# One section of the modulation weights by eight small transfers

## The chip, the cores and the metric

The kernel runs on one core of a Trainium2 chip. The metric is device time in microseconds of one execution. Before the change the median of three runs is 667.86 us (667.57 to 667.94).

## The reference

One decode step of a block with adaptive layernorm, for 4 rows (B = 4) of 512 values, all inputs in bf16. Attention has 32 heads of 128 over a cache of 4096 positions; the cache (K and V, 4 x 32 x 4096 x 128 each) is nearly all of the 283 MB read.

```
mod = silu(c) @ w_mod                       # w_mod: 512 x 3072, six sections of 512 columns
sa, ca, ga, sb, cb, gb = the six sections   # 4 x 512 each
h = layernorm(x) * (1 + ca) + sa
x = x + ga * (softmax((h @ wq) K^T / sqrt(128)) V @ wo)
h = layernorm(x) * (1 + cb) + sb
z = gelu(h @ w_in)                          # w_in: 512 x 1792
z1, z2 = halves of z;  z2 = layernorm(z2)
out = x + gb * ((z1 * (w_sp * z2 + b_sp)) @ w_out)   # w_out: 896 x 512
```

Section 4 of w_mod, cb, is the scale of the second norm.

## The kernel before

The 128 pairs of row and head are taken in 32 steps of four heads of one row. A step loads 4 MB of K and 4 MB of V, each partition holding 128 consecutive positions of one head. VectorE multiplies K by the query in two halves (mult, L288), PE sums over the head's dimension by matmuls with an identity (reduce_d, L294), VectorE finishes the scores (sum8 and scores), ScalarE takes the exponential (L326), PE multiplies with V two steps later (pv, L366). K tiles ("kt") and V tiles ("vt") have two buffers each. The schedule is manual: every engine takes its instructions in the order of the code.

All large loads are issued by SyncE in the order of the code, and its queue holds them in that order:

- at the start wq (L89), five sections of w_mod into wm_sb (L92), K of steps 0 and 1, V of step 0;
- in step i, K of step i+2 (load_k) and V of step i (load_v; V of step 1 is loaded in step 0), through the helper's line L104;
- after step 2's V: the four parts of wo (L581) and wo_last (L586), into the pool wts, which takes the memory of the pool pre (wq and wm_sb) when that is closed;
- in step 30: the last V in five parts (L104), win_sb (L597), wout_sb (L599, in wts) and the gate's section of w_mod, section 5 (L602), which goes into a buffer of the V tiles.

Small loads (c, x, and w_sp and b_sp into sp_t) are issued by ScalarE.

Before step 0, c is turned into columns by four transposes on PE (rows_to_cols, L187), silu is computed on these columns (L226 to L234) into cT, and mod_cols (L242) multiplies sections 0 and 1 of w_mod with cT for the first norm. In step 2, mod_cols multiplies sections 2, 3 and 4 (ga, sb, cb) into modT (L573). In step 5, the scalars of w_sp and b_sp are spread (L589 to L591) and 1 is added to cb (L593).

After the last step come the output projection, the second norm, the two halves of gate with win_sb (L684), the product with wout_sb (L707), the gate's section (L715), and one store (L753).

Of the kernel before, what the change touches and what calls it, by code (L numbers as in the profile page):

```python
# [8 lines left out]
BF16 = mybir.dt.bfloat16  # L9
F32 = mybir.dt.float32  # L10
AF = mybir.ActivationFunctionType
ALU = mybir.AluOpType
# [12 lines left out]
def kernel(  # L25
# [16 lines left out]
    nc = tc.nc  # L42
    P = 128
    B, _, D = A_x.shape
    _, H, SK, DH = A_k_cache.shape
    F = B_w_in.shape[1]
    FH = F // 2
    DJ = D // P
    NF = F // P
    NH = FH // P  # L50
    NJ = SK * HQ // P
# [13 lines left out]
    consts = ctx.enter_context(tc.tile_pool(name="consts", bufs=1))  # L65
    kvp = ctx.enter_context(tc.tile_pool(name="kv", bufs=2))
# [6 lines left out]
    def ps_sm(shape, dtype=F32):  # L73
        return psum.tile(shape, dtype, name="sm", bufs=3)
# [6 lines left out]
    pre = pre_cm.__enter__()  # L81
    c_sb = pre.tile([B, D], BF16, name="c_sb")
# [4 lines left out]

    wq_sb = pre.tile([P, DJ, H * DH], BF16, name="wq_sb")
    nc.sync.dma_start(out=wq_sb, in_=A_wq.rearrange("(p j) n -> p j n", p=P))  # L89
    wm_sb = pre.tile([P, DJ, 5 * D], BF16, name="wm_sb")  # L90
    wm = w_mod.rearrange("(p j) n -> p j n", p=P)
    nc.sync.dma_start(out=wm_sb, in_=wm[:, :, 0:5 * D])  # L92

    def kv_view(cache, i):
        g, b = divmod(i, B)
# [16 lines left out]
    def load_v(i):  # L112
# [8 lines left out]
    ident_bf = consts.tile([P, P], BF16, name="ident_bf")  # L121
# [13 lines left out]

    st2 = consts.tile([P, 2, DJ + 1], F32, name="st2")
    nc.vector.memset(st2, 0.0)
    nc.vector.memset(st2[:, 1, DJ:], LN_EPS * D / P)

# [3 lines left out]
        out=sel32, in_=ident_f.rearrange("p (q r) -> p r q", r=R), axis=AX.X, op=ALU.add  # L143
# [10 lines left out]
    for g in range(G):  # L154
        nc.vector.tensor_reduce(out=selg[:, g:g + 1], in_=idr[:, g], axis=AX.XY, op=ALU.add)
    nc.vector.tensor_reduce(
        out=sel4, in_=ident_f.rearrange("p (c b) -> p b c", b=B), axis=AX.X, op=ALU.add
# [3 lines left out]
        out=mask8, in_=ident_f.rearrange("p (h u) -> p h u", h=2 * HQ), axis=AX.X, op=ALU.add  # L161
# [3 lines left out]
    x1w = consts.tile([P, DJ, R], F32, name="x1w")  # L165
    nc.gpsimd.memset(x1w, 0.0)
    cT = consts.tile([P, DJ, B], BF16, name="cT")

    consts.tile([P, 512], mybir.dt.uint8, name="gap")
    wk.tile([P, 32], mybir.dt.uint8, name="gap", bufs=1)  # L170
    pbds, opss = [], []
    for k in range(3):
        t = consts.tile([P, NJ, HQ], BF16, name=f"pbd{k}")
        nc.gpsimd.memset(t, 0.0)
        pbds.append(t)
    for k in range(2):
        t = psum.tile([P, G, DH], F32, name=f"ops{k}", bufs=1)
# [3 lines left out]
    def bc(ap, n):  # L181
        return ap[:, None, :].to_broadcast([P, n, ap.shape[-1]])

    def rows_to_cols(src):
        t = ps_sm([P, DJ, B], BF16)
        for j in range(DJ):
            nc.tensor.transpose(t[:, j, :], src[0:B, j:D:DJ], ident_bf[0:B, 0:B])  # L187
        return t

    def across(rhs, mat):  # L190
# [13 lines left out]
    def normed(pool, src, name, then=None, last=None):  # L204
# [16 lines left out]
        rsqrt(rs, v, 1.0, eps)  # L221
        return xc, rs

    cps = rows_to_cols(c_sb)
    cx = pre.tile([P, DJ, B], F32, name="cx")
    nc.vector.tensor_copy(out=cx, in_=cps)  # L226
    sg = pre.tile([P, DJ, B], F32, name="sg")
    nc.vector.tensor_scalar(
        out=sg, in0=cx, scalar1=-60.0, scalar2=-1.0, op0=ALU.max, op1=ALU.mult
    )  # L230
    nc.scalar.activation(out=sg, in_=sg, func=AF.Exp)
    nc.vector.tensor_scalar_add(out=sg, in0=sg, scalar1=1.0)
    nc.vector.reciprocal(out=sg, in_=sg)
    nc.vector.tensor_tensor(out=cT, in0=cx, in1=sg, op=ALU.mult)  # L234

    def mod_cols(s0, n, dst):

        for m in range(n):
            s, j = divmod(m, DJ)
            c0 = (s0 + s) * D + j  # L240
            for k in range(DJ):
                nc.tensor.matmul(  # L242
                    dst[:, m, :], lhsT=wm_sb[:, k, c0:c0 + (P - 1) * DJ + 1:DJ], rhs=cT[:, k, :],
                    start=(k == 0), stop=(k == DJ - 1),
                )
# [11 lines left out]
        out=hs, in0=modA[:, DJ:2 * DJ, :], scalar=1.0, in1=xn, op0=ALU.add, op1=ALU.mult  # L257
# [174 lines left out]
    for n in set(SETS):  # L432
        picks[n] = consts.tile([P, n, P], BF16, name=f"pick{n}")
        for a in range(n):
            u = P // n
            nc.vector.tensor_copy(
                out=picks[n][:, :, a * u:(a + 1) * u],
                in_=ident_bf.rearrange("p (u r) -> p r u", r=n),
# [77 lines left out]
        nc.vector.tensor_tensor(out=a, in0=a, in1=wp, op=ALU.add)  # L516

    modT = consts.tile([P, 3 * DJ, B], F32, name="modT")

    g8 = consts.tile([P, 2, B], F32, name="g8")  # L520
    sp_t = consts.tile([1, 2], BF16, name="sp_t")
# [8 lines left out]
    for i in range(NT):  # L530
        more = list(QPLAN.get(i, ()))
        mult(i, 0)
        if i >= 1:
            scores(i - 1)
        if i >= 2:
            norm_b(i - 2)
        add_up()
        rows_up()
        dealt()
        if i >= 3:  # L540
            o_pick(i - 3)
        reduce_d(i, 0)
        if i >= 3:
            o_cols(i - 3)
        if more:
            queries(more.pop(0))
        mult(i, 1)
        if i >= 1:
            norm_r(i - 1)
        if i >= 3:  # L550
            o_scale(i - 3)
        sum8(i, 0)
        reduce_d(i, 1)
        load_k(i + 2)
        if i >= 1:
            norm_a(i - 1)
        project()
        if i - 3 in ends:
            deal(ends[i - 3])
        while more:  # L560
            queries(more.pop(0))
        if i >= 2:
            pv(i - 2)
        if i == 0:
            load_v(1)
        elif 2 <= i < L:
            load_v(i)
        if i == 2:
            nc.scalar.dma_start(out=sp_t[:, 0:1], in_=B_w_sp[0:1, 0:1])
            nc.scalar.dma_start(out=sp_t[:, 1:2], in_=B_b_sp.rearrange("(a b) -> a b", b=1))  # L570
            mps = ps_sm([P, 3 * DJ, B])
            mod_cols(2, 3 * DJ, mps)
            nc.vector.tensor_copy(out=modT, in_=mps)  # L573
            pre_cm.__exit__(None, None, None)
            wts = tl = ctx.enter_context(tc.tile_pool(name="wts", bufs=1))
            wo_sb = wts.tile([P, H - HQ, D], BF16, name="wo_sb")
            wo_last = wts.tile([P, HQ, D], BF16, name="wo_last")
            hl = (H - HQ) * DH
            h0 = 0
            for n in SETS:  # L580
                nc.sync.dma_start(  # L581
                    out=wo_sb[:, h0:h0 + n, :],
                    in_=A_wo[h0 * DH:(h0 + n) * DH].rearrange("(p r) n -> p r n", p=P),
                )
                h0 += n
            nc.sync.dma_start(out=wo_last, in_=A_wo[hl:H * DH].rearrange("(q p) n -> p q n", p=P))  # L586
        if i == 5:
            sps = ps_sm([P, 2])
            nc.tensor.matmul(sps, lhsT=ones_b, rhs=sp_t, start=True, stop=True)  # L589
            nc.vector.tensor_copy(out=spf, in_=sps)  # L590
            nc.vector.tensor_copy(out=g8[:, 1, :], in_=spf[:, 0:1].to_broadcast([P, B]))  # L591
            cbT = modT[:, 2 * DJ:3 * DJ, :]
            nc.vector.tensor_scalar_add(out=cbT, in0=cbT, scalar1=1.0)  # L593
        if i == L - 1:
            load_v(L)
            win_sb = wts.tile([P, DJ, F], BF16, name="win_sb")
            nc.sync.dma_start(out=win_sb, in_=B_w_in.rearrange("(p j) n -> p j n", p=P))  # L597
            wout_sb = wts.tile([P, NH, D], BF16, name="wout_sb")
            nc.sync.dma_start(out=wout_sb, in_=B_w_out.rearrange("(j p) n -> p j n", p=P))  # L599
            wg_sb = kvp.tile([P, NJ, DH], BF16, name="vt", bufs=2)  # L600
            wg_sb = wg_sb.rearrange("p n d -> p (n d)")[:, 0:DJ * D].rearrange("p (k n) -> p k n", k=DJ)
            nc.sync.dma_start(out=wg_sb, in_=wm[:, :, 5 * D:])  # L602

    gaT = modT[:, 0:DJ, :]
# [24 lines left out]
    def sums():  # L629
# [21 lines left out]
        out=nv2, in0=mq2[:, 0:1], scalar=mq2[:, 0:1], in1=mq2[:, 1:2],  # L651
        op0=ALU.mult, op1=ALU.subtract,
# [6 lines left out]
        out=hl, in0=xs, scalar=mq2[:, 0:1], in1=cbT[:, :, BL], op0=ALU.subtract, op1=ALU.mult  # L659
    )  # L660
    nc.vector.scalar_tensor_tensor(
        out=hT2[:, :, BL], in0=hl, scalar=rsl, in1=sbT[:, :, BL], op0=ALU.mult, op1=ALU.add
# [4 lines left out]
        out=x1m, in0=x1[:, :, :, None].to_broadcast([P, DJ, B, HQ]),  # L667
        in1=mask4[:, None, None, :].to_broadcast([P, DJ, B, HQ]), op=ALU.mult,
    )
    x1r = ps_sm([B * DJ, P])  # L670
    for k in range(DJ):
        nc.tensor.matmul(
            x1r[:, k:P:DJ], lhsT=x1m[:, k].rearrange("p b j -> p (b j)"), rhs=sel32,
            start=True, stop=True,
# [4 lines left out]
    def gate(h):  # L679
# [21 lines left out]
        out=zz.rearrange("p f g b -> p g b f"), in0=z1[:, None].to_broadcast([P, 2, B, NH]),  # L701
        in1=st3[:, 0:2], op=ALU.mult,
    )
    y = ps_q()[:, 0:DJ * 2 * B].rearrange("p (j g b) -> p j g b", j=DJ, g=2)
    for j in range(DJ):
        for f in range(NH):
            nc.tensor.matmul(  # L707
                y[:, j], lhsT=wout_sb[:, f, j * P:(j + 1) * P], rhs=zz[:, f],
                start=(f == 0), stop=(f == NH - 1),
# [3 lines left out]
    for j in range(DJ):  # L713
        for k in range(DJ):
            nc.tensor.matmul(  # L715
                gb[:, j, :], lhsT=wg_sb[:, k, j * P:(j + 1) * P], rhs=cT[:, k, :],
                start=(k == 0), stop=(k == DJ - 1),
# [3 lines left out]
        out=mq3, in_=ps3.rearrange("p (g b f) -> p g b f", g=2, b=B), axis=AX.X, op=ALU.add  # L721
# [4 lines left out]
        out=rs3, in0=mq3[:, 1], scalar=LN_EPS, in1=rs3, op0=ALU.add, op1=ALU.subtract  # L726
# [3 lines left out]
        out=g8[:, 0, :], in0=mq3[:, 0, :], scalar=-1.0, in1=g8[:, 1, :], op0=ALU.mult, op1=ALU.mult  # L730
# [5 lines left out]
        out=t3[:, 2], in0=yb[:, 0], scalar1=spf[:, 1:2], scalar2=None, op0=ALU.mult  # L736
    )
    nc.vector.tensor_tensor(
        out=g8, in0=g8, in1=rs3[:, None, :].to_broadcast([P, 2, B]), op=ALU.mult
    )  # L740
    nc.vector.tensor_tensor(
        out=t3[:, 0:2], in0=g8[:, :, :, None].to_broadcast([P, 2, B, DJ]), in1=yb, op=ALU.mult
# [3 lines left out]
        out=tt, in_=t3.rearrange("p g b j -> p b j g"), axis=AX.X, op=ALU.add  # L746
# [37 lines left out]
```

## Time and profile before

| | before |
|---|---|
| median of three runs | 667.86 us (667.57 to 667.94) |
| span of the profiled execution, first to last instruction | 665.8 us |
| the profiled execution's own time | only its span is recorded; 667.86 - 665.8 = 2.1 us lie around it if it ran like the median |
| busy PE / VectorE / ScalarE | 399.3 / 419.5 / 85.0 us |
| DMA | 283.15 MB, mean 425 GB/s |
| mean granted TensorE clock | 0.828 |

A row of the page's groups gives line, engine, operation, output and inputs with shapes, the count, then the busy time in us, the mean ns of one, and the idle time just before with what ended most of it. A row of a timeline begins with start and duration in us. A row of the waits gives who waited for whom: total us, times, longest. "SPq" is SyncE's queue, where a DMA_DIRECT2D is the issue of one load.

### The profile page before, as it was taken

The numbers are of one execution on the slowest core, as the hardware profiler recorded it, in microseconds if no ns is written. First come the engines' busy times: TensorE is split into PE (matmuls) and PEld (weight loads), VectorE is DVE, ScalarE is ACT, GpSimd is POOL, SyncE is SP. The second block draws the span as 40 slices with busy tenths as digits, with TensorE's granted clock in tenths as the row PEclk, the third lists the DMA queues.
The fourth block names the chain that finished last, engine by engine and source line by source line (L and its number), as shares of the span: only waits on it lengthen the run. The fifth ranks groups of instructions, "written<-read, shape, count | busy, mean of one in ns | idle before, by whom it ended". The sixth has DMA issues, their size and how long they took to land.

```text
span 665.8 us, 6509 instructions
## 1 busy us (share of the span) xinstructions
PE 399.3 (60%) x2674; PEld 175.4 (26%) x2674; DVE 419.5 (63%) x589; ACT 85.0 (13%) x278; POOL 3.8 (1%) x17
## 2 busy tenths in 40 slices
PE   1195795556556746754665467566555468666675
PEld 0132331222222312222222222222222223322245
DVE  3485592776565777655567756657765566776833
ACT  1021120111011111101111110111111011111112
POOL 1000000000000000000000000000000000000000
PEclk9998987777898778789877778787777897887975
DMA  8999999999999999999999999999999999999996
GB/s 363 452 419 433 431 417 435 436 437 422 439 432 438 422 439 433 436 423 436 435 431 426 438 435 432 426 436 437 431 426 437 435 429 432 433 436 421 438 419 234
DMA packets 13377, 283.15 MB, mean 425 GB/s; under 512 B 1308, under 2 KB 3236, under 8 KB 4132
## 3 DMA queue, kind: packets, MB, share of 16 engines
q1 hardware_dynamic: 13328, 282.73, 98.9%
q8 instruction: 21, 0.34, 0.2%
q14 instruction: 8, 0.07, 0.0%
q10 hardware_dynamic: 20, 0.01, 0.0%
HBM read 282.73 MB, written 0.00 MB: 425 GB/s over the span
## 4 chain that ended last, share of the span: by engine, by line
DMA 56%; DVE 28%; PE 13%; issue 1%; SPq 1%; ACT 0%; DVEq 0%
DMA kt<-in_A_k_cache_dram 52%; DVE kt L288 21%; PE red L294 11%; DMA win_sb<-in_B_w_in_dram 5%; DVE osb L378 2%; DVE S L303 1%; DVE mrow L312 1%; DVE osb L374 1%; PE ops L366 1%; SPq L104 1%; DVE mt L316 1%; DVE nM L318 0%; PE qps L274 0%; DVE mb L314 0%; DVE nM L319 0%
## 5 line engine op out<-in xcount | busy, mean ns | idle before, releaser
L294 PE MATMUL red<-kt,ident_bf 128*128 128x512 bf16 x1024 | 301.5, 461 | 236.4 <-DVE kt L288 236.4
L288 DVE TENSOR_TENSOR kt<-kt,qbc 128x8192 bf16<-128x8192 bf16 x64 | 282.8, 4420 | 185.2 <-DMA kt<-in_A_k_cache_dram 184.2
L294 PEld LDWEIGHTS <-ident_bf 128*128 128x128 bf16 x1024 | 118.9, 116 | 411.5 <-issue 285.8
L326 ACT ACTIVATE pbd<-S,nM 32x128 bf16<-32x128 f32 x128 | 73.8, 577 | 505.3 <-DVE nM L319 463.2
L366 PE MATMUL ops<-vt,pbd 128*16 128x512 bf16 x992 | 62.6, 388 | 1.4 <-DMA vt<-in_A_v_cache_dram 1.4
L303 DVE TENSOR_REDUCE S<-red 128x64 f32<-128x512 f32 x64 | 43.8, 684 | 5.8 <-PE red L294 5.8
L378 DVE SCALAR_TENSOR_TENSOR osb<-ops,selg,osb 128x128 f32<-128x128 f32 x93 | 32.6, 351 | 3.3
L326 ACT ACTIVATION_READ_ACCUMULATOR pbd<-S,nM 32x1 f32 x128 | 32.0, 250 | 0.0
L366 PEld LDWEIGHTS <-pbd 128*16 128x16 bf16 x992 | 23.2, 90 | 30.7 <-issue 8.5
L386 PEld LDWEIGHTS sm<-sel,osb 128*128 128x128 f32 x62 | 11.7, 194 | 7.4 <-issue 2.2
L374 DVE TENSOR_SCALAR osb<-ops,selg 128x128 f32<-128x128 f32 x31 | 10.1, 325 | 5.3 <-PE ops L366 5.3
L386 PE MATMUL sm<-sel,osb 128*128 128x4 f32 x62 | 9.2, 219 | 2.1 <-DVE osb L378 2.0
L278 ACT CAST qbc<-qps 128x512 bf16<-128x512 f32 x8 | 4.7, 585 | 45.3 <-PE qps L274 45.3
L274 PE MATMUL qps<-wq_sb,hTb 128*32 128x512 bf16 x128 | 9.2, 412 | 1.6 <-DVE hTb L262 0.9
L312 DVE TENSOR_REDUCE mrow<-S 128x1 f32<-128x128 f32 x32 | 9.2, 286 | 1.1
L242 PE MATMUL sm<-cT,wm_sb 128*128 128x4 bf16 x80 | 3.0, 173 | 8.3 <-DMA wm_sb<-in_w_mod_dram 8.3
L316 DVE STREAM_TRANSPOSE mt<-mb 128x32 f32<-128x32 f32 x32 | 6.8, 212 | 1.1
L337 DVE TENSOR_SCALAR rsb<-mask,rs 128x4 f32<-128x4 f32 x32 | 7.2, 224 | 0.4 <-ACT pbd L326 0.4
L318 DVE TENSOR_REDUCE nM<-mt 128x1 f32<-128x32 f32 x32 | 6.0, 186 | 1.1
L314 DVE COPY mb<-mrow 128x32 f32<-128x32 f32 x32 | 5.8, 181 | 1.1
L491 PE MATMUL sm<-wo_sb,od 128*4 128x512 bf16 x24 | 5.7, 379 | 0.0
L319 DVE TENSOR_SCALAR nM<-nM 128x1 f32<-128x1 f32 x32 | 4.9, 153 | 1.1
(136 smaller groups left out, 88.8 us busy)
## 6 DMA issues: line engine op xcount, KB each, us to landing
kt<-in_A_k_cache_dram SPq DMA_DIRECT2D x31, 4096.0 KB, 23.0
vt<-in_A_v_cache_dram SPq DMA_DIRECT2D x31, 4096.0 KB, 30.7
wq_sb<-in_A_wq_dram SPq DMA_DIRECT2D x1, 4096.0 KB, 12.3
kt<-in_A_k_cache_dram SPq DMA_DIRECT2D x2, 2048.0 KB, 16.7
wo_sb<-in_A_wo_dram SPq DMA_DIRECT2D x3, 1024.0 KB, 22.9
kt<-in_A_v_cache_dram SPq DMA_DIRECT2D x3, 1024.0 KB, 25.5
wm_sb<-in_w_mod_dram SPq DMA_DIRECT2D x1, 2560.0 KB
win_sb<-in_B_w_in_dram SPq DMA_DIRECT2D x1, 1792.0 KB
```

The costliest lines, as they stand in the source:

```text
L274: nc.tensor.matmul(qp[R * q:R * (q + 1)], lhsT=hTb[:, k, b, :], rhs=wq_v[:, k, gs, q, :], start=(k == 0), stop=(k == DJ - 1), tile_positio ...
L288: nc.vector.tensor_tensor(out=kt, in0=kt, in1=bc(qbc[:, g, b, :], KC), op=ALU.mult)
L294: nc.tensor.matmul(red, lhsT=ident_bf, rhs=kt[:, :, m * RD:(m + 1) * RD], start=(m == 0), stop=(m == DH // RD - 1),)
L303: nc.vector.tensor_reduce(out=st[i, "S"][:, kc * KC:(kc + 1) * KC], in_=st.pop((i, "red", kc)), axis=AX.X, op=ALU.add,)
L312: nc.vector.tensor_reduce(out=mrow, in_=S, axis=AX.X, op=ALU.max)
L316: nc.vector.transpose(mt, mb)
L326: nc.scalar.activation(out=pbd[r, :, q], in_=S[r, :], func=AF.Exp, bias=nM[r, :], scale=att_scale, accum_out=rs[r, :],)
L337: nc.vector.tensor_scalar(out=st[g, "rsb"][:, b, :], in0=mask4, scalar1=st.pop((i, "rs")), scalar2=None, op0=ALU.mult)
L366: nc.tensor.matmul(opss[i % 2][g:g + G * HQ], lhsT=pbds[i % 3][:, n, :], rhs=vts[i][:, n, :], start=(m < 4), stop=(m >= NJ // G - 4), tile ...
L374: nc.vector.tensor_scalar(out=osb, in0=ops[:, 0, :], scalar1=selg[:, 0:1], scalar2=None, op0=ALU.mult)
L378: nc.vector.scalar_tensor_tensor(out=osb, in0=ops[:, g, :], scalar=selg[:, g:g + 1], in1=osb, op0=ALU.mult, op1=ALU.add,)
L386: nc.tensor.matmul(op, lhsT=st.pop((i, "osb")), rhs=sel4, start=True, stop=True)
```

## The change

Section 4 of w_mod (cb) is no longer part of the first load, which takes four sections. It is loaded after wo_last in step 2 into w8, a tile of 64 partitions with eight rows of w_mod each, by eight transfers; each fills eight partitions that lie four apart (partition 32h + r + 4e, for h = 0, 1 and r = 0 to 3). Its product with silu(c) moves to step 5: 32 matmuls that contract over 64 partitions, with a second set of columns of silu(c), cT8, of that layout. For this silu is computed on the rows of c before the transposes, of which there are now 4 + 8. In step 2 mod_cols does 8 column groups instead of 12. wout_sb moves from wts into the same buffer of the V tiles as the gate's section.

```diff
+    P2 = P // 2
+    K8 = D // P2
...
-    wm_sb = pre.tile([P, DJ, 5 * D], BF16, name="wm_sb")
+    wm_sb = pre.tile([P, DJ, 4 * D], BF16, name="wm_sb")
     wm = w_mod.rearrange("(p j) n -> p j n", p=P)
-    nc.sync.dma_start(out=wm_sb, in_=wm[:, :, 0:5 * D])
+    nc.sync.dma_start(out=wm_sb, in_=wm[:, :, 0:4 * D])
...
-    cps = rows_to_cols(c_sb)
-    cx = pre.tile([P, DJ, B], F32, name="cx")
-    nc.vector.tensor_copy(out=cx, in_=cps)
-    sg = pre.tile([P, DJ, B], F32, name="sg")
+    sg = pre.tile([B, D], F32, name="sg")
...
-    nc.vector.tensor_tensor(out=cT, in0=cx, in1=sg, op=ALU.mult)
+    cs = pre.tile([B, D], BF16, name="cs")
+    nc.vector.tensor_tensor(out=cs, in0=c_sb, in1=sg, op=ALU.mult)
+    nc.vector.tensor_copy(out=cT, in_=rows_to_cols(cs))
+    nc.vector.tensor_copy(out=cT8, in_=rows_to_cols(cs, K8))
...
         if i == 2:
...
-            mps = ps_sm([P, 3 * DJ, B])
-            mod_cols(2, 3 * DJ, mps)
-            nc.vector.tensor_copy(out=modT, in_=mps)
+            mps = ps_sm([P, 2 * DJ, B])
+            mod_cols(2, 2 * DJ, mps)
+            nc.vector.tensor_copy(out=modT[:, 0:2 * DJ], in_=mps)
...
             nc.sync.dma_start(out=wo_last, in_=A_wo[hl:H * DH].rearrange("(q p) n -> p q n", p=P))
+
+            w8 = wts.tile([P2, K8, D], BF16, name="w8")
+            w8v = w_mod[:, 4 * D:5 * D].rearrange("(h e s j) n -> h s e j n", h=2, e=8, s=4)
+            for h in range(2):
+                for r in range(4):
+                    nc.sync.dma_start(out=w8[32 * h + r:32 * h + 32:4], in_=w8v[h, r])
         if i == 5:
...
-            cbT = modT[:, 2 * DJ:3 * DJ, :]
-            nc.vector.tensor_scalar_add(out=cbT, in0=cbT, scalar1=1.0)
+            mp8 = ps_sm([P, DJ, B])
+            for j in range(DJ):
+                for k in range(K8):
+                    nc.tensor.matmul(
+                        mp8[:, j, :], lhsT=w8[:, k, j:D:DJ], rhs=cT8[:, k, :],
+                        start=(k == 0), stop=(k == K8 - 1),
+                    )
+            nc.vector.tensor_scalar_add(out=cbT, in0=mp8, scalar1=1.0)
         if i == L - 1:
...
-            wout_sb = wts.tile([P, NH, D], BF16, name="wout_sb")
+            ends_sb = kvp.tile([P, NJ, DH], BF16, name="vt", bufs=2).rearrange("p n d -> p (n d)")
+            wout_sb = ends_sb[:, 0:NH * D].rearrange("p (f n) -> p f n", f=NH)
             nc.sync.dma_start(out=wout_sb, in_=B_w_out.rearrange("(j p) n -> p j n", p=P))
-            wg_sb = kvp.tile([P, NJ, DH], BF16, name="vt", bufs=2)
-            wg_sb = wg_sb.rearrange("p n d -> p (n d)")[:, 0:DJ * D].rearrange("p (k n) -> p k n", k=DJ)
+            wg_sb = ends_sb[:, NH * D:(NH + DJ) * D].rearrange("p (k n) -> p k n", k=DJ)
             nc.sync.dma_start(out=wg_sb, in_=wm[:, :, 5 * D:])
```

More of the change, by code (lines that the diff above doesn't have):

```diff
@@ L167 @@
     cT = consts.tile([P, DJ, B], BF16, name="cT")
+    cT8 = consts.tile([P2, K8, B], BF16, name="cT8")
     consts.tile([P, 512], mybir.dt.uint8, name="gap")
@@ L182, in bc, with rows_to_cols @@
         return ap[:, None, :].to_broadcast([P, n, ap.shape[-1]])
[L184 to L187, printed above, removed]
+    def rows_to_cols(src, n=DJ):
+        t = ps_sm([D // n, n, B], BF16)
+        for j in range(n):
+            nc.tensor.transpose(t[:, j, :], src[0:B, j:D:n], ident_bf[0:B, 0:B])
         return t
@@ L222, in normed @@
         return xc, rs
-    cps = rows_to_cols(c_sb)
-    cx = pre.tile([P, DJ, B], F32, name="cx")
-    nc.vector.tensor_copy(out=cx, in_=cps)
-    sg = pre.tile([P, DJ, B], F32, name="sg")
+    sg = pre.tile([B, D], F32, name="sg")
     nc.vector.tensor_scalar(
-        out=sg, in0=cx, scalar1=-60.0, scalar2=-1.0, op0=ALU.max, op1=ALU.mult
+        out=sg, in0=c_sb, scalar1=-60.0, scalar2=-1.0, op0=ALU.max, op1=ALU.mult
     )
@@ L518 @@
     modT = consts.tile([P, 3 * DJ, B], F32, name="modT")
+    cbT = modT[:, 2 * DJ:3 * DJ, :]
     g8 = consts.tile([P, 2, B], F32, name="g8")
```

## The prediction

> **What bounds the kernel now.** I read the page first (queues, chain of waits, groups), then SyncE's timeline and its waits, then the last stretch of the timeline, and last the trace's packet and landing records, which are quoted in sentences. The page, queues, chain and group of the large multiply:
>
> ```profile
> q1 hardware_dynamic: 13328, 282.73, 98.9%
> q8 instruction: 21, 0.34, 0.2%
> ...
> DMA 56%; DVE 28%; PE 13%; issue 1%; SPq 1%; ACT 0%; DVEq 0%
> ...
> L288 DVE TENSOR_TENSOR kt<-kt,qbc 128x8192 bf16<-128x8192 bf16 x64 | 282.8, 4420 | 185.2 <-DMA kt<-in_A_k_cache_dram 184.2
> ```
>
> One DMA queue fills 98.9% of the span on 16 engines, and VectorE spends 184.2 us waiting for K. The packet records agree: a 32 KB packet takes 1.213 us, and each engine starts the next one where the last ended. So a change in what the engines carry, or a gap in their feed, reaches the end; compute is mostly cover. SyncE's timeline, then its waits, both in extracts:
>
> ```profile
> 80.58 0.39 SPq L586 DMA_DIRECT2D wo_last<-in_A_wo_dram  x1
> 94.21 0.34 SPq L104 DMA_DIRECT2D kt<-in_A_k_cache_dram  x1
> 96.06 0.33 SPq L104 DMA_DIRECT2D vt<-in_A_v_cache_dram  x1
> 109.74 0.33 SPq L104 DMA_DIRECT2D kt<-in_A_k_cache_dram  x1
> ...
> 633.50 0.38 SPq L599 DMA_DIRECT2D wout_sb<-in_B_w_out_dram  x1
> 643.22 6.26 SPq L602 DMA_DIRECT2D vt<-in_w_mod_dram  x1
> ```
>
> ```profile
> SPq L602 <- DMA vt<-in_A_v_cache_dram: 9.3, 1, 9.3
> ...
> SPq L599 <- DMA vt<-in_A_v_cache_dram: 7.1, 1, 7.1
> ...
> SPq L586 <- DMA sp_t<-in_B_w_sp_dram: 0.3, 1, 0.3
> ```
>
> The three waits are the important find. wout has a fresh buffer, yet waits 7.1 us for a V load it has nothing to do with. The landing records explain it: the loads take eight completion semaphores in turn (100, 102, 103, 106 to 110), and a load is not issued before the previous load on its semaphore, eight loads earlier, has landed whole. V of step 29 landed at 633.5, V of step 30 at 643.2, the first sp_t at 80.6, on the semaphores of wout, w_mod's gate and wo_last: three cases, each within 0.05 us. The last stretch:
>
> ```profile
> 657.78 1.65 PE L684 MATMUL red<-hT,win_sb 128*128 128x4 bf16 x56 [0.78 <-DMA win_sb<-in_B_w_in_dram]
> 660.15 0.89 PE L707 MATMUL qps<-zz,wout_sb 128*128 128x8 bf16 x28 [0.20 <-DVE zz L700]
> 661.38 0.58 PE L715 MATMUL sm<-cT,vt 128*128 128x4 bf16 x16 [0.34 <-DMA vt<-in_w_mod_dram]
> 663.14 0.37 SPq L753 DMA_DIRECT2D out_dram<-xo  x1
> ```
>
> The end hangs on the landing of win_sb, and almost as much on w_mod's gate 3.6 us later; what the slowest DMA engine loses is lost at the end. Which engine is that? The 21 instruction packets (q8, 16 KB each) fall, in the packet records, on only eight of the engines, in turn; each holds its engine's stream back by 1.42 us. The engine that finishes win_sb last took three after 107 us (113.7, 411.6, 654.9); it began K of step 5 at 106.5. The next is 0.31 us earlier, and the last of the other eight engines, held up by smaller instruction packets (8 KB, q14), 0.43 us earlier.
>
> **The change, part by part.** Times are the profile's; its span is 665.8 us, the median 667.86, so about 2.1 us lie around it, which I hold fixed.
>
> 1. *w_mod is loaded with four sections, not five.* An engine's 32 packets of 5 KB took 196 ns each, 6.2 us; 4 KB packets (wo_sb's last load) took 159 ns, 5.0 us. With the pitch (3 ns less than a packet) that is 1.2 us less on every engine before K arrives. The first multiply at 28.96 waits for K, and the next K loads follow without a gap, so the shift passes on: -1.2.
>
> 2. *The eight small loads themselves.* c and x, of four partitions, complete in the records by four increments, sp_t of one by one, full loads by sixteen; so eight partitions use eight engines, and each gets eight times eight 1 KB rows. The pitch of such rows in the tail is 42.4 ns: 64 x 42.4 = 2.7 us. Of x's four engines at least three are among those that q8 never hits, so I put the load on those eight: +2.7 - 1.2 = +1.5 there, -1.2 on the other eight. The last of the loaded half was 0.43 behind the end: +1.1 at the end at least. [...]
>
> 3. *What they do to SyncE's queue.* They stand after wo_last and ahead of K of step 5. By the round of eight, they wait in turn for the second sp_t, K 4, V 2 (landed 98.0), the four wo loads (100.4, 102.9, 105.3, 106.6) and wo_last (107.9). Queued behind them are K 5 (94.21 before, now not before 107.9) and V 3. With the shift of 1.2 the eighth goes out at 106.7, takes 0.39 (L586's row), and K 5, which needs the first small load landed (about the same time), goes out at 107.1. By then wo_last has left the unloaded engines at 104.8 to 106.3, and the loaded ones finish near 107.6 to 109.0. So the DMA runs dry, eight engines at least. What a restart costs, two places show. At the start, wq was issued at 0.73 into idle engines; first packets came at 1.84 to 2.77, and with their longer first packet the stream counted from 1.65 to 2.27 us after the issue. At K 4 (74.02), five engines had run dry, amid full traffic: 3.06 to 3.85. So K 5 streams from 108.7 to 109.3, or from 110.1 to 110.9. For the engine that ends last that is +2.2 to +2.9, or +3.6 to +4.4, against 106.5. Its three fetches remain. I take +2.7: nearer the start's row, since these engines are empty as they were there. This includes part 1, and covers part 2, since the loaded half restarts about then too.
>
> 4. *silu on rows* (512 elements in 4 partitions): five VectorE and ScalarE steps at about 0.6 to 0.7 (the 128x512 cast at L278 takes 0.58, the reduce at L303 0.68) and eight more transposes (four took 0.29) put about 4 us ahead of x's layernorm, whose result was ready at 11.9 and waited for w_mod until 19.2. Cost 0; without that cover up to 4.
>
> 5. *Sixteen fewer mod matmuls at i=2* (48 took 1.76): -0.6 on PE, but VectorE's next multiply at 78.55 waits for K 3 anyhow: 0. *32 matmuls in i=5:* 1.23 by the same line's 32 at 19.23. VectorE's add at 135.94, in order ahead of mult(6,0), waits for them to about 137.1; mult(6,0) waited for K 6 until 137.30: 0, with 0.2 left, and a miss is absorbed, as K 7 needn't flow before 147.
>
> 6. *wout in the V buffer* waits for pv(29), 637.23 + 1.90 = 639.1, not 633.5. Its packets flow from 653 on: 0. Were the tile waited for whole, L707 would wait for the gate's landing, 660.15 to 661.4: up to +1.2. Against it: the five parts of the last V, one tile, are consumed as each lands. I take 0.
>
> Sum: +2.7, giving 667.86 + 2.7 = 670.6 us.
>
> **Rivals.**
> - *No dry spell* (K 5 isn't held back): parts 1 and 2 alone. The loaded half ends last: +1.1, 669.0. Against it: the three waits of the round of eight.
> - *A balance that pays, not slower:* the small loads go to the engines without instruction fetches, the others shed 1.2 us, and the end follows those: 666.6. It needs no dry spell, and a loaded half that ends at least 2.7 us (1.5 + 1.2) ahead of the other. For it: q8 does fall on one half only, and of the loaded half seven engines end win_sb 3.3 us or more ahead. Against it: the eighth, which four q14 packets hit (200.1, 355.9, 516.4, 655.0), is just 0.43 ahead; those packets would have to fall elsewhere.
> - *A slow restart*, as at K 4: +4, 671.9.
> [...]
>
> **How the numbers follow.** Dry spell, near the start's row 0.50; slow restart 0.22; no dry spell 0.14; the balance that pays 0.11; fixed cost 0.03. A measurement here tells about 0.2% (1.3 us) from no change. Slower by more: both restarts and the fixed cost, and the part of "no dry spell" in which the tile of part 6 is waited for whole: 0.76. Within: 0.17, the rest of "no dry spell" and that part of the paying balance that stays at its -1.2. Faster: 0.07, the paying balance with something gained beside it. The range leaves out the fixed cost and the paying balance: from 667.6 (no dry spell, and one q8 packet of 1.42 fewer on the last engine) to 672.4 (slow restart, its upper end and a little for part 6).
>
> **What would show it.** SyncE: K 5 issued near 107 instead of 94.2, after a chain of waits for V 2, wo and wo_last; V 3 right behind. A dip of DMA share between 105 and 111 where there was none (1.03 from 99.8 to 116.5). VectorE's multiply of step 5 at about 120.5 instead of 117.97; afterwards every wait for K shifted by the same 2 to 3 us, and L684 starting near 660.5 with the tail after it unchanged. Wrong if K 5 still goes out at 94, if the multiply of step 5 comes earlier than 118, or if L707 waits for the gate's load.

## The result and the profile after

The changed kernel takes 673.71 us (median of 4 runs, 673.25 to 674.69) against 667.72 (4 runs, 667.28 to 667.94): a ratio of 1.0092, 95% interval 1.0080 to 1.0104, or +6.0 us where +2.7 was forecast. The profiled execution took 673.43 us, its span is 671.7, so 1.7 us lie around it.

The page of the kernel after, its queues, chain and the large multiply:

```profile
q1 hardware_dynamic: 13904, 282.73, 98.5%
q8 instruction: 21, 0.34, 0.2%
...
DMA 59%; DVE 29%; PE 10%; issue 1%; SPq 0%; ACT 0%; DVEq 0%
...
L291 DVE TENSOR_TENSOR kt<-kt,qbc 128x8192 bf16<-128x8192 bf16 x64 | 282.8, 4420 | 190.8 <-DMA kt<-in_A_k_cache_dram 189.8
```

The multiply is as long as before to the tenth; VectorE waits 5.6 us more for K. So the loss is in the DMA stream, and the queue's share has fallen only from 98.9% to 98.5%. SyncE's timeline of the kernel after, from step 2 on and around the last loads:

```profile
78.63 0.43 SPq L590 DMA_DIRECT2D wo_last<-in_A_wo_dram  x1
81.19 26.76 SPq L596 DMA_DIRECT2D w<-in_w_mod_dram  x8
108.06 0.37 SPq L106 DMA_DIRECT2D kt<-in_A_k_cache_dram  x1
108.53 0.37 SPq L106 DMA_DIRECT2D vt<-in_A_v_cache_dram  x1
109.01 0.37 SPq L106 DMA_DIRECT2D kt<-in_A_k_cache_dram  x1
...
643.75 0.38 SPq L616 DMA_DIRECT2D vt<-in_B_w_out_dram  x1
647.79 6.22 SPq L618 DMA_DIRECT2D vt<-in_w_mod_dram  x1
```

Its waits between 76 and 120 us:

```profile
SPq L596 <- DMA vt<-in_A_v_cache_dram: 4.7, 1, 4.7
SPq L596 <- DMA wo_sb<-in_A_wo_dram: 2.8, 3, 1.8
SPq L596 <- DMA sp_t<-in_B_b_sp_dram: 2.1, 1, 2.1
...
SPq L596 <- DMA wo_last<-in_A_wo_dram: 0.7, 1, 0.7
```

The eight small loads spread over 26.8 us of SyncE's time, each behind the load eight places earlier: the second sp_t, K 4, V 2, the wo loads, wo_last. The waits make 10.3 us of that. The issue of the first small load alone takes 10.5 us, which no semaphore explains, but it ends before V 2 lands and so holds nothing up. The last four go out at 102.07, 104.56, 105.91 and 107.28, each within 0.02 us of the landing of the load eight places ahead. K 5 (the K load of step 5), issued at 94.21 before, goes out behind them at 108.06. The DMA share of the window 104 to 112 is 0.82, against 1.05 before (two rows of the windows view, after and then before):

```profile
104.00:112.00 8.00, 6.55 (x47) 2.66 (x45) 0.00 (x0) 0.00 (x0) 0.00 (x0) 0.77 0.82 279
```

```profile
104.00:112.00 8.00, 7.67 (x49) 3.00 (x47) 0.00 (x0) 0.00 (x0) 0.00 (x0) 0.68 1.05 436
```

That is the dry spell. Step 5's multiply shows its price, after and then before:

```profile
121.43 4.42 DVE L291 TENSOR_TENSOR kt<-kt,qbc 128x8192 bf16<-128x8192 bf16 x1 [18.32 <-DMA kt<-in_A_k_cache_dram]
```

```profile
117.97 4.43 DVE L288 TENSOR_TENSOR kt<-kt,qbc 128x8192 bf16<-128x8192 bf16 x1 [13.98 <-DMA kt<-in_A_k_cache_dram]
```

It is 3.5 us late. But there the loss should have stopped growing, and it did not: the second multiplies of steps 6, 18, 24 and 31 are 3.6, 3.9, 4.4 and 4.5 us late, and win_sb's landing, which starts L700, 5.8 (L684 before the change):

```profile
663.60 1.66 PE L700 MATMUL red<-hT,win_sb 128*128 128x4 bf16 x56 [1.90 <-DMA win_sb<-in_B_w_in_dram]
666.02 0.91 PE L723 MATMUL qps<-zz,vt 128*128 128x8 bf16 x28 [0.26 <-DVE mq L736]
667.42 0.59 PE L731 MATMUL sm<-cT,vt 128*128 128x4 bf16 x16 [0.49 <-DMA vt<-in_w_mod_dram]
669.00 0.37 SPq L769 DMA_DIRECT2D out_dram<-xo  x1
```

A multiply waits for the last of the 16 engines (a 4 MB load lands by sixteen increments in the landing records), and its lateness jumps from step to step (3.2 us at step 8, 4.9 at step 20). The landing of the engine that ends first shows the trend evenly: 3.84 us late at K 5, 5.50 at K 31, a little more with almost every load.

The packet records say where this comes from. A 32 KB packet took 1.213 us before, almost without exception. After, half of them take 1.215 and a fifth 1.222 (mean after 140 us, instruction fetches included, 1.2181 against 1.2144), and this from the first loads on: early 4 MB loads land 9.710 us apart, before 9.681. So a second cause works from the start, and has nothing to do with the small loads.

What could it be? The change adds cT8, 8 x 4 values of two bytes, 64 bytes in each partition, to the pool in front of the K and V buffers. In the program's allocation all that lies behind moves by 64 bytes, from a multiple of 512 to 64 past one. The kernel before has an unused tile of 512 bytes in that pool (`consts.tile([P, 512], mybir.dt.uint8, name="gap")`), with which the experiments shift the buffers at will.

### The profile page after: what moved, and what is told of

Same layout as the page of the kernel before. It is cut to its first block, busy times and chain, and to the rows that moved or that the text cites. A ratio compares the mean times of both kernels' runs of the same rounds, so it can differ in the third digit from the quotient of the medians.

```text
span 671.7 us, 6571 instructions
## 1 busy us (share of the span) xinstructions
PE 398.4 (59%) x2698; PEld 176.4 (26%) x2698; DVE 423.7 (63%) x590; ACT 85.4 (13%) x278; POOL 3.8 (1%) x17
## 3 DMA queue, kind: packets, MB, share of 16 engines
q1 hardware_dynamic: 13904, 282.73, 98.5%
## 4 chain that ended last, share of the span: by engine, by line
DMA 59%; DVE 29%; PE 10%; issue 1%; SPq 0%; ACT 0%; DVEq 0%
DMA kt<-in_A_k_cache_dram 53%; DVE kt L291 22%; PE red L297 10%; DMA vt<-in_A_v_cache_dram 3%; DMA vt<-in_w_mod_dram 3%; DVE osb L381 2%; DVE S L306 2%; DVE mrow L315 1%; DVE osb L377 1%; DVE mt L319 1%; DVE nM L321 0%; DVE mb L317 0%; DVE nM L322 0%; PE ops L369 0%; DVE qbc L513 0%
## 5 line engine op out<-in xcount | busy, mean ns | idle before, releaser
L190 PE MATMUL sm<-ident_bf,cs 4*64 4x4 bf16 (+1 forms) x12 | 1.3, 228 | 10.3 <-DVE cs L235 10.3
```

## The experiments

All were timed in five rounds beside the kernel before, whose median was between 667.46 and 667.70 us. Differences are of medians.

**The start address alone**, b_shift64, in the kernel before:

```diff
-    consts.tile([P, 512], mybir.dt.uint8, name="gap")
+    consts.tile([P, 576], mybir.dt.uint8, name="gap")
```

> The kernel before with its unused 512-byte tile made 576 bytes, so that the K and V buffers and all behind them start 64 bytes later, as they do after the change (64 instead of 0 past a multiple of 512). Theory A (the start address of the buffers sets the pace of the packets): in the trace after, a 4 MB load takes 9.711 us from the first loads on, against 9.681 before, so 0.030 us for each of 67 loads' worth: +2.0 us, about 669.7, and 32 KB packets of 1.215 to 1.222 instead of 1.213. Rival B (the pace is slower because the engines run in step after the dry spell): no change, 667.7.

670.64 us, +3.1 (ratio 1.0044, 1.0030 to 1.0058). 52% of the 32 KB packets after 140 us took 1.215 us, 20% 1.222. The multiply's row on the page, where before VectorE waited 184.2 us for K:

```profile
L288 DVE TENSOR_TENSOR kt<-kt,qbc 128x8192 bf16<-128x8192 bf16 x64 | 282.8, 4420 | 188.4 <-DMA kt<-in_A_k_cache_dram 187.5
```

There is no dry spell in this kernel (K 5 goes out at 94.85, and the DMA share from 104 to 112 is 1.10), so rival B falls. The size is above the expected 2.0: the mean packet is longer by 3.9 ns, and 504 of them on each engine make 2.0 us. Smaller packets grew too, together by 0.5 us per engine; most of it is the 1 KB rows, of which a tenth take 55 ns or more, against 46 before. Some 0.6 us stay open.

**The change with the address put back**, a_aligned, in the kernel after:

```diff
-    consts.tile([P, 512], mybir.dt.uint8, name="gap")
+    consts.tile([P, 448], mybir.dt.uint8, name="gap")
```

> The kernel after with its unused tile made 448 bytes, so that K and V start where they did before; cT8 takes the 64 bytes. Theory A: the pace returns to 9.681 us per load and 2.0 us are won back, about +4.0 over before, 671.7; K 5 still goes out near 107.8 and its multiply starts near 121. Rival B: nothing is won back, +6.0, 673.7.

670.01, +2.4 (1.0041, 1.0028 to 1.0053): 3.6 of the 6.0 us won back by leaving out 64 unused bytes, and nearly all 32 KB packets at 1.213 again. The engine that ends first is now 3.22 us late at K 5 and 3.19 at K 31: the growth is gone. SyncE's timeline of this kernel still has K 5 behind the small loads:

```profile
81.91 25.48 SPq L596 DMA_DIRECT2D w<-in_w_mod_dram  x8
107.51 0.37 SPq L106 DMA_DIRECT2D kt<-in_A_k_cache_dram  x1
```

In the packet records of this kernel every engine begins its first packet of K 5 at 108.5 to 108.8 on the timeline's zero, 1.0 to 1.3 us after the issue; that packet is longer than the usual 1.21, and counted back from its end by 1.21 the stream stands from 109.2 to 109.7, 1.7 to 2.2 us after the issue (1.65 to 2.27 forecast). This kernel is the change as the prediction saw it.

**Which addresses are slow**: b_shift256 and b_shift128, the tile of 512 bytes made 768 or 640, in the kernel before.

> As b_shift64, with the buffers moved by 256 bytes. Theory A1 (the pace needs a start at a multiple of 512 bytes): 32 KB packets over 1.213 us and +2 to +3 us, as b_shift64. Theory A2 (a smaller multiple, up to 256, is enough): 1.213 us and no change, 667.6.

> As b_shift256, moved by 128 bytes. Theory A3 (256 bytes are the step that counts): slower packets, +2 to +3, 670. Theory A4 (128 bytes are enough): no change, 667.6.

256 bytes: 667.46, -0.1 (0.9997, 0.9989 to 1.0006), packets at 1.213. 128 bytes: 670.69, +3.2 (1.0045, 1.0033 to 1.0058), packets from 1.213 to 1.221. So A2 and A3 hold as far as these offsets show: 256 bytes past a multiple of 512 is as fast here as 0, 64 or 128 past one is not. The tile moves everything behind it, but the 32 KB packets go into the K and V buffers and wq alone. The mean 32 KB packet is 0.3% longer at 64 and at 128 (1.2183 and 1.2185 us against 1.2144), so that twice the offset does not lengthen it twice as much: what makes the packets longer is not shown.

**The wait alone**, b_tiny8, in the kernel before, behind wo_last; the data are read by nobody, and w_mod is loaded whole:

```diff
+            t8 = wts.tile([8, 8, 32], BF16, name="t8")
+            for r in range(8):
+                nc.sync.dma_start(out=t8[:, r], in_=w_mod[8 * r:8 * r + 8, 0:32])
```

> The kernel before with eight loads of 8 partitions by 64 bytes (4 KB in all, read by nobody) behind wo_last; w_mod is loaded whole as before. Theory C: the wait alone makes the dry spell, without the bytes and without the shift by the smaller first load: K 5 goes out near 108.3 instead of 94.2, and the time rises by 4 to 5 us, to about 672. Rival D': a dry spell needs the 512 KB on half of the engines; 4 KB cost at most 0.3, 668.0.

671.60, +4.0 (1.0061, 1.0049 to 1.0074), with 4 KB of data. K 5 goes out at 108.41, and the DMA share from 104 to 112 is 0.75. A fixed time for each small load can't be the reason, as the next run shows.

**Four instead of eight**, b_tiny4: the same with range(4).

> As b_tiny8, with four loads of 8 partitions by 64 bytes instead of eight. Theory C: the eighth load before K 5 is now the second wo load, which lands near 103; K 5 goes out near 103 instead of 108.4, before wo_last has left the engines, the DMA doesn't run dry, and the time is that of before within 0.3 (667.6 to 667.9). Rival D: small loads cost by their number; half of b_tiny8's +4.0, 669.6.

667.67, +0.15 (1.0001, 0.9992 to 1.0010). SyncE's timelines, b_tiny8 and then b_tiny4:

```profile
83.41 24.89 SPq L589 DMA_DIRECT2D t<-in_w_mod_dram  x8
108.41 0.36 SPq L104 DMA_DIRECT2D kt<-in_A_k_cache_dram  x1
```

```profile
81.97 18.64 SPq L589 DMA_DIRECT2D t<-in_w_mod_dram  x4
102.83 0.36 SPq L104 DMA_DIRECT2D kt<-in_A_k_cache_dram  x1
```

With four, K 5 waits for the second wo load and goes out at 102.83. That is 8.6 us later than before, and free; in my reading wo's last loads still keep the engines busy, since in the kernel before wo_last's sixteen increments come only from 106.30 to 107.86. Not the number of transfers costs, but that eight in a row hold the next large load until everything ahead of them has landed.

**Eight in another place**, a_later_aligned: in a_aligned, the eight loads stand under `if i == 3:`, behind V 3.

> As a_aligned, with all eight small loads one step later, behind K 5 and V 3, ahead of K 6. Theory C (the round of eight, wherever eight loads stand in a row): K 5 goes out at 93 to 95 and its multiply comes at 117, but now the eighth small load waits for V 3 and K 6 behind it goes out only near 126.5 instead of 108; the DMA runs dry there, and the loss of a_aligned comes back one step later: +2.4, 670.0. Rival G (the loss belongs to the place behind the wo loads, whose small packets leave the engines uneven): it goes away, to a_split_aligned's +1.5 or less.

670.10, +2.6 (1.0041, 1.0028 to 1.0053). Its timeline:

```profile
93.51 0.33 SPq L106 DMA_DIRECT2D kt<-in_A_k_cache_dram  x1
95.35 0.33 SPq L106 DMA_DIRECT2D vt<-in_A_v_cache_dram  x1
97.17 29.91 SPq L597 DMA_DIRECT2D w<-in_w_mod_dram  x8
127.19 0.37 SPq L106 DMA_DIRECT2D kt<-in_A_k_cache_dram  x1
```

K 5 is free again, at 93.51; now K 6 is held until V 3 has landed. Step 5's second multiply is 1.2 us early, step 7's 3.3 late. The loss went with the eight loads, as the round of eight semaphores has it.

**The loads without the dry spell**, a_split_aligned: in a_aligned, four loads stay and four go under `if i == 3:`.

> As a_aligned, with four of the eight small loads where they were and the other four one step later, behind V 3. Theory C (the round of eight semaphores holds K 5 back until wo_last has landed, and the DMA runs dry): with four, K 5 waits for the second wo load only and goes out near 102.5, the DMA doesn't run dry, and the loads cost what their bytes cost: +1.1, about 668.8; if the other half of the engines sets the end, down to -1.0. Rival D (each small load has a cost of its own, wherever it stands): it stays at +3 or more, 670.7 or more.

669.13, +1.5 (1.0026, 1.0015 to 1.0037, which is +1.0 to +2.5); the 1.1 of parts 1 and 2 lies inside. K 5 goes out at 103.11, and the DMA share from 104 to 112 is 1.09: no dry spell. The profiled execution, at 670.95, was the slowest of the seven.

**Is it the one-sided load?** a_one16_aligned loads the section by one transfer of 64 partitions; a_half_aligned loads half of it by four one-sided transfers, the rest by one of 32 partitions; a_full16_aligned loads it like wo_last:

```diff
-    P2 = P // 2
+    P2 = P
...
-            for h in range(2):
-                for r in range(4):
-                    nc.sync.dma_start(out=w8[32 * h + r:32 * h + 32:4], in_=w8v[h, r])
+            w8w = w_mod[:, 4 * D:5 * D].rearrange("(p j) n -> p j n", p=P)
+            nc.sync.dma_start(out=w8, in_=w8w)
```

> As a_aligned, with the section loaded by one transfer of 64 partitions, which uses all 16 engines. Theory E (of what a_split_aligned loses, 1.5 us, the load on one half of the engines is the cause): each engine carries as many bytes as before, 32 rows of 1 KB for a fifth of 5 KB packets, +0.1 to +0.2 us, no dry spell: 667.7. Rival F (what a_split_aligned loses comes from the later layout and the product in step 5): it stays near +1.5, 669.1.

> As a_split_aligned, but the second half of the section is one transfer of 32 partitions (16 engines), one step later, so that only half as much is put on one half of the engines: 32 + 16 rows of 1 KB there (2.0 us, less 1.2), 16 on the other half (0.7, less 1.2). Theory E: about half of a_split_aligned's loss, +0.7, 668.3. Rival F: the same as a_split_aligned, 669.1; a gain from a better balance would show as less than 667.6.

> As a_aligned, with the section loaded by one transfer of 128 partitions and 4 rows each, as wo_last is, and multiplied in step 5 by 16 matmuls over 128 partitions. Theory E (what a_split_aligned loses comes from the load on one half of the engines): every engine carries the bytes of before, 32 rows of 1 KB at 42 ns instead of 1 KB more on 32 packets at 38 ns: +0.1 to +0.2, 667.7; rows take 46 ns, against 79 to 116 ns in a_one16_aligned, where 16 engines write 64 partitions. Rival F (the product in step 5, silu on rows, or wout in the V buffer cost it): +1 or more, 668.6.

a_one16_aligned: 671.01, +3.5 (1.0056, 1.0041 to 1.0071), and a_half_aligned: 670.71, +3.2 (1.0044, 1.0031 to 1.0057). Both missed by 2 us and more, and neither tells E from F, because a new cost came in: in the packet records of a_one16_aligned a 1 KB row into the 64 partitions takes 0.07 to 0.12 us, median 0.089, against 0.046, and K packets in flight beside them up to 2.9 us instead of 1.2. The rows add 1.3 us per engine and the longer K packets 1.5, 2.8 of the 3.5 us. So 16 engines on these partitions take twice as long for a row, while the eight engines of the change kept 46 ns; why is not shown. In a_half_aligned's records some 100 rows are slow, which is 0.2 us per engine, but the 32 KB packets in flight from 123 to 129 us, when its second half is written by 16 engines into 32 partitions, are longer too, by 1.7 us per engine. That makes 1.9 of its 3.2 us; with the +0.7 that theory E forecast, 0.6 stay open.

a_full16_aligned: 667.59, +0.1 (1.0004, 0.9995 to 1.0013), rows at 46 ns. With silu on rows, the product in step 5 and wout in the V buffer all in place, nothing is lost. So rival F falls. What a_split_aligned loses beside it, 1.4 us, goes with the eight one-sided transfers. Four small transfers alone cost 0.15 (b_tiny4), so I put it down to the load on one half of the engines; no run has eight transfers, no dry spell and an even load, which would show it.

**Both together**, b_tiny8_shift64: the two edits of b_tiny8 and b_shift64.

> The kernel before with both mechanisms and nothing else of the change: the eight loads of 64 bytes per partition of b_tiny8, and the 64 bytes of b_shift64. Theory H (the two add up): 4.0 + 3.1 = +7.1, 674.6; with the 1.2 us that the smaller first load wins, that would be the +6.0 of the kernel after. Rival I (they overlap, or a third part of the change costs time): clearly less than +6, or, if the sum with the 1.2 falls short of 6.0, a part is still missing.

674.08, +6.4 (1.0095, 1.0078 to 1.0112; +5.2 to +7.5). The sum of the two, 7.1, lies inside. Less the 1.2 us of the smaller first load, 5.2 remain of the change's 6.0. The 0.8 between them lies within the interval, so that theory H stands, but a further part of that size (rival I) isn't excluded. None of the twelve versions beats the kernel before clear of noise.

## Why the prediction was wrong in size

- **The step that failed: a term that was missing.** The sum had no entry for where the buffers lie. The prediction costed cT8's transposes and matmuls, not its 64 bytes, and so put the move of the K and V buffers at nothing without a reason. b_shift64 measures that omission at +3.1, and a_aligned, against the kernel after, at 3.6. Without it the sum holds: +2.7 forecast, +2.4 measured (a_aligned, +1.9 to +3.5). So close a match is partly luck: K 5's stream began 0.4 to 0.5 us later than forecast, which by the prediction's own count from 106.5 would be +2.7 to +3.2.
- **Part 3, the round of eight and the dry spell**, was right in its mechanism and nearly in its numbers: K 5 at 107.1 forecast, 107.51 in a_aligned and 108.06 in the kernel after; its stream from 108.7 to 109.3 forecast, from 109.2 to 109.7 in a_aligned. The eighth small load went out at 106.72 there (106.7 forecast), but its issue took 0.67 us and not L586's 0.39. The restart, 1.7 to 2.2 us from issue to stream, went like wq's at the start (1.65 to 2.27), not like K 4's (3.06 to 3.85), so that the rival with the slow restart falls.
- **Part 1**: the first multiply came at 27.64 in a_aligned, 1.3 us early (1.2 forecast), and at 27.99 in the kernel after, where the slower packets had already eaten some of it.
- **Part 2**, at least +1.1 by the load on half of the engines: +1.5 in a_split_aligned (+1.0 to +2.5). In the kernel after each small load has eight increments as its packets land, besides one near its issue; the first small load's come from 105.91 to 107.62. The rival "a balance that pays" falls with it; that the engine hit by four q14 packets sets the end was read from the trace before and not tested by itself.
- **Part 4**: the estimate of 0.6 to 0.7 per step was wrong for one: the reciprocal of 4 x 512 values took 3.34 us in the kernel after. That x's layernorm was ready 3.4 us later, near the forecast 4, is luck: before the change VectorE had idled 2.57 us for x's transposes, and that gap was filled. The cover held: PE still waited 3.88 us for w_mod.
- **Part 5**: the 32 matmuls took 1.23 as forecast, and step 6's multiply still waited 0.40 us for K 6. **Part 6**: wout was issued at 643.75, and L723 started 1.4 us ahead of the gate's load; cost 0, as said.
- **The rival "no dry spell"**: K 5 was held back. **The fixed cost**, with a chance of 0.03: no run shows a fixed time for each small load; four of them together cost 0.15 us (b_tiny4).
- **The sign that would have shown it**: a shift that stays the same after step 5. It grew by 2.4 us from step 5's multiply to win_sb's landing (3.46 to 5.82; on the engine that ends first from 3.84 to 5.88), which is how the missing term was found.

## What to carry to other kernels

A new small tile moves every buffer behind it (the 64 bytes alone cost 3.1 us in b_shift64). Where DMA sets the time, look first at where the large buffers start (here 0 and 256 past a multiple of 512 were fast, 64 and 128 slow), and compare the length of single packets before and after (here 1.2144 and 1.2181 us on the mean). The loads here took eight semaphores in turn; a run of eight small ones made the next large load wait until all that stood ahead had landed (K 5 at 108.41 in b_tiny8, +4.0 us), while four cost nothing (K 5 at 102.83 in b_tiny4, +0.15). What I put down to loading one half of the engines more is 1.4 us here beside an even load. The trace before suggests why, though no run tested it: the load's end is set by the last engine, and one of the loaded half ended only 0.43 us ahead of it already.

## What the runs showed that I had not expected

- A DMA into buffers that start 64 or 128 bytes past a multiple of 512 moves 32 KB packets in 1.2183 and 1.2185 us on the mean, against 1.2144 at 0 and 256: +3.1 and +3.2 us on 667.5.
- Sixteen engines writing 64 partitions need 0.089 us for a 1 KB row (median), eight engines on the same partitions 0.046, and K packets in flight beside them take up to 2.9 us instead of 1.2.
- A reciprocal of 512 values per partition takes 3.34 us, 6.5 ns a value, where a multiply of the same shape takes 0.68 us.
